# One table of letters for the order within 342 rounds, and the convolution in four streams

## The chip, the core and the metric

The kernel runs on one core of one Trainium2 chip. The metric is the device time of one execution in microseconds (us). Five engines work on their own instruction lists in a fixed order each and wait for one another by semaphores: TensorE (PE in the profile, its weight loads PEld), VectorE (DVE), ScalarE (ACT), GpSimd (POOL) and SyncE (SP). POOL, SP and ACT also issue DMA transfers. Since the lists are fixed when the program is built, an instruction that waits holds up all that stands behind it on its engine.

## The reference

Two independent results stand side by side in the output, over the same 2048 positions and 576 channels.

```python
# A: a state-space convolution. K has 576 filters of 2048 taps, summed over 128 states
P = exp(dt * (A_re + 1j * A_im)[:, :, None] * arange(L))
K = einsum("dn,dnl,dn->dl", C, P, dt * B).real
y = irfft(rfft(pad(u)) * rfft(pad(K)))[:L] + u * Dskip
# B: attention, 32 query heads of 18 with one key and one value head
q, k, v = x @ wq, x @ wk, x @ wv
o = softmax(q k^T * 18 ** -0.5) v
out = concatenate([y, o @ wo], axis=-1)
```

## The kernel before

**Attention.** The 2048 queries are cut into 4 chunks c of 512, the 32 heads into 16 pairs, the 2048 keys into 16 blocks kb of 128. One *tile* of scores is one head-pair member, one key block and one chunk: two matmuls (`s`, in half precision, K = 55) fill 128 x 1024 numbers of PSUM, ACT takes their exponentials in one instruction (`P`), and PE multiplies them by the values into `ops`, 8 instructions that the program calls a *product* being half of what two tiles need. There are 1024 tiles, `pairs` in the code, three PSUM buffers for scores (`NS = 3`) and eight buffers for exponentials (`NP = 8`). A *round* is three tiles; there are 342. Scores come from `scores`, exponentials from `exponentials`, products from `product`.

**What else PE does** is put between the products of the rounds, in pieces: the query projections (`q`, with the bound `up`), the output projections (`op`), and the convolution's groups. All of these use one PSUM bank, `ps_f`, the *filler bank*: a group must be evacuated by DVE before the next may start.

**The convolution** goes through 12 chunks k of 48 channels. `front(k)` makes the filters: DVE works out angles and decays, ACT takes sines and exponentials, and the tables `tab` give the taps by matmuls `kg`, evacuated to `ksb`. Sines need another table of functions on ACT than exponentials, so they are taken for two chunks at once: six *sine blocks*, the first before the loop and five within it, each of four sine instructions and two table loads. What the second chunk needs is parked in DRAM (`park<-two`) and loaded again. `back(k)` transforms the input (`hu`, `lu`) and the filter (`hk`, `lk`) by matmuls with `dft_sb`, multiplies the transforms on DVE in eight products and six additions (`acc`, `pt`), adds parts by accumulating DMAs on POOL's queue, recombines them (`sv`, `w`), transforms back (`iy`) and adds u times Dskip. Two streams run at a time: `back(k)` and `front(k + 1)`; `turn` starts the next two when both have ended.

**What sets the order.** The program is built by Python generators. `fill` is called before scores are due. It lets the streams (`prep`, `side` for projections, `conv`) take a step each while a credit lasts, which a planner works out from some twenty constants; the clock that it reads has one time each for PE, DVE and ACT, and guesses DMA landings as fixed spans (`K.t + 6.0`). The lines that decide:

```python
spare = credit - LEAST
if st is side and not (urgent or late or side.holds):
    spare -= SLOPE * max(ahead, 0.0)
elif st is side and side.holds:
    spare += HOLD
wait = then - K.t - (GAP_NEW if st is side and not urgent and not side.holds else GAP)
if st.go(self.step, max(spare, wait), holder()):
    more = True
    break
```

Behind the last tile, `conv.drain()` issues whatever is left of the convolution, and `finish` normalises the last heads (`rc_last`), ends the last output projection (`fin`) and stores it.

Of the kernel before, what the change touches and what calls it, by code (L numbers as in the profile page):

```python
# [25 lines left out]
KT = [(k * 128, 128) for k in range(5)]  # L26
DT = KT[:4] + [(512, 64)]
# [11 lines left out]
LIMIT = 60.0  # L39

# [5 lines left out]
RATE = 6.983  # L46
PACE = 1.7672
AHEAD = 0.4952
TOTAL = 604.4861
LAST = 813.2825  # L50
DEFER = 0.378
NAUG = 5
LEFT = 1.1655
CAP = 1.5491
DEBT = 0.6604
GROUP = 0.1377
HOLD = 0.3071
LEAD = 1.8204
MOST = 0.4269
LEAST = 0.3048  # L60
NEAR = 1.3779
SLOPE = 0.851
SOON = 1.3672
URGENT = 8.8421
BACK = 2
HELD = 0
GAP = 0.2663
GAP_NEW = 0.3191
# [13 lines left out]

class Clock:
# [6 lines left out]
    def __init__(self):  # L90
        self.t = self.v = self.a = 0.0
        self.work = 0.0
        self.s = [0.0] * NS
        self.fill = 0.0
        self.due = self.last = 1e9

    def near(self):

        return NEAR if self.t + SOON > min(self.due, self.last) else 0.0

    def pe(self, cost, *after):
        self.t = max(self.t, *after) + cost if after else self.t + cost

    def act(self, cost, after=0.0):
        self.a = max(self.a, after) + cost
        return self.a

    def filled(self):

        self.fill = self.v + 0.25  # L110
        self.due = 1e9

    def dve(self, n, rate, after):
        cost = 0.068 + rate * n + (0.119 if after else 0.0)
        self.v += cost
        self.work += cost


class Vector:
# [5 lines left out]
    def cost(self, rate, out, *ins, n=None):  # L125

        place = lambda x: (x.name, x.offset)
        self.k.dve(math.prod((n or out).shape[1:]), rate, self.last in [place(x) for x in ins if hasattr(x, "offset")])
        self.last = place(out)
# [9 lines left out]
    def tensor_scalar(self, out, src, *a, **k):  # L139
        self.cost(0.527e-3, out, src, *a)  # L140
# [18 lines left out]
class Stream:  # L159
# [26 lines left out]
    def go(self, step, credit, lock=None):  # L186

        k = self.k
        ready = self.ready if self.kind != "p" or self.holds else max(self.ready, k.fill)
        if not self.live or self.kind == "b" or self.kind == "p" and (credit <= 0 or k.t < ready or lock not in (None, self)):  # L190
            return False
        if self.kind == "v" and (k.t < self.ready or k.v > k.t + self.ahead - k.near()):
            return False
# [16 lines left out]
class Attention:  # L210
# [7 lines left out]
    def __init__(self, tc, ctx, aps, clock):  # L218
        self.tc, self.nc, self.a, self.k = tc, tc.nc, aps, clock
# [15 lines left out]
    def bank(self, n, name):  # L235
        self.k.pe(0.0, self.k.fill)
# [10 lines left out]
    def setup(self, tp, conv):  # L247
# [4 lines left out]
        self.sel = conv.con[:, 2 * NF:]  # L252
# [122 lines left out]
    def second(self):  # L375
# [3 lines left out]
        K.pe(0.86)  # L379
        self.last()  # L380
        K.pe(0.86)
        K.v = max(K.v, K.t)
# [6 lines left out]
    def maxima(self):  # L389
# [4 lines left out]
        K.pe(1.1)  # L394
        K.v = max(K.v, K.t)
# [4 lines left out]
    def values(self):  # L400
# [4 lines left out]
        K.pe(1.0)  # L405
        K.v = max(K.v, K.t)
# [8 lines left out]
    def qproj(self, c, m, xt):  # L415
# [5 lines left out]
        for f in range(n // 256):  # L421
            sl = slice(f * 256, f * 256 + 256)
            yield "p", K.fill, False
            ps = self.bank(256, f"q{c}_{m}_{f}")
            for k in range(5):
# [6 lines left out]
                K.pe(0.465)  # L432
                self.q_left -= 1
                self.units += 1
                K.due = K.t + 0.465 * (4 - k)
                if k < 4:
                    yield "p", 0.0, True
            K.v = max(K.v, K.t)
# [21 lines left out]
    def queries(self, c, m, qh, ql, aw):  # L460
# [18 lines left out]
        yield "p", max(K.v + 0.4, K.fill), False  # L479
# [10 lines left out]
        K.pe(0.15)  # L490
        K.v = max(K.v, K.t + 0.3)
# [33 lines left out]
    def scores(self, i, c, pr, kb, cost):  # L525
# [7 lines left out]
        K.pe(cost, K.s[i % NS])  # L533
        return ps, K.t + 0.27

    def exponentials(self, i, c, pr, kb, ps, ready, free):
        nc, K = self.nc, self.k
        K.s[i % NS] = K.act(0.925, max(ready, free)) + 0.1
# [7 lines left out]
    def gather(self, c, g, o_ps):  # L546
        nc = self.nc
        o_sb = self.p2.tile([P, CT], F32, tag="o", name=f"o{c}_{g}", bufs=1)
        self.k.v = max(self.k.v, self.k.t)
        self.V.tensor_copy(o_sb, o_ps)  # L550
        self.o_free = self.k.v + 0.3
        nc.sync.dma_start(self.od[c][g * P:(g + 1) * P, :], o_sb)

    def normalize(self, c, ms):
# [11 lines left out]
        yield "v", K.t + 6.0, False  # L566
# [6 lines left out]
        yield "v", K.v + 3.0, False  # L573
# [8 lines left out]
        for m in ms:  # L582
            mn = MT[m][1]
            yield "v", K.t + 5.0, False
            V.tensor_tensor(o[:mn, m, :], o[:mn, m, :], tiles[m][:mn, :], op=ALU.mult)
            self.scaled[m] = K.v + 0.3
# [3 lines left out]
    def outproj(self, c):  # L590
        nc, V, K = self.nc, self.V, self.k
        o = self.oT
        self.o_left += 40
        yield "p", max(self.scaled[4], K.fill), False
# [183 lines left out]
    def main(self, conv, flag):  # L778
# [81 lines left out]
        for r in range(0, len(pairs), NS):  # L860
# [45 lines left out]
            if r:  # L906
                fill(free())
# [643 lines left out]
```

## Time and profile before

| what | value |
|---|---|
| median of 3 runs | 1216.06 us (1213.11 to 1217.59) |
| the profiled execution | 1217.0 us, span 1215.2 us |
| busy PE / ACT / DVE / POOL | 1099.6 / 1035.3 / 961.1 / 95.5 us |
| mean granted clock of TensorE | 0.973 |
| DMA, all queues | 117.87 MB, mean 97 GB/s |

The span goes from the first to the last instruction of the profiled execution; the execution's own time is 1.8 us longer. An engine's busy time is the union of its instructions; matmuls overlap, and a PE that is busy is not PE at its peak. "Idle before" a group is the time that its engine stood still just ahead of it, with the one it waited for. A windows row gives, for one stretch, its length, the busy time and instruction count of each engine, the granted share of the TensorE clock, the share of the DMA engines and the rate.

### The profile page before, as it was taken

Reading aid. Unit: us, or ns where it says so; the run is one execution under the profiler, and the core shown is the slowest. Engines: PE = TensorE matmul, PEld = TensorE weight load, DVE = VectorE, ACT = ScalarE, POOL = GpSimd, SP = SyncE. Lnnn points to the kernel's source line nnn. Section 1 sums busy time; section 2 is a strip of 40 time slices with the busy share of each in tenths; the row PEclk is TensorE's granted clock in tenths of the full one; section 3 lists DMA queues with packets and bytes.
Section 4 is the critical chain, followed back from the end, with each engine's and each line's share of the span. In section 5 each row is a group of like instructions: output and inputs, shape, how many; then the busy total and the mean of one; then the engine's idle time right before and its main releaser. Section 6 shows DMA issues by size and latency. Waiting matters only on the chain. (4 is left out here: it accounts for less than half of the span.)

```text
span 1215.2 us, 41325 instructions
## 1 busy us (share of the span) xinstructions
PE 1099.6 (90%) x17974; PEld 534.7 (44%) x17974; DVE 961.1 (79%) x1722; ACT 1035.3 (85%) x1092; POOL 95.5 (8%) x151
## 2 busy tenths in 40 slices
PE   7999999899999899999989999986789998999924
PEld 2454454345445344545444545432344543454412
DVE  7868979977975885995989596873779589869875
ACT  5899899899889978999999999999689999999700
POOL 1010201110110100110010000020000000000000
PEclk9999999999999999999999999998899999999967
DMA  8432343343323324322341312232042124241122
GB/s 295 130 121 69 105 118 90 113 134 110 91 58 97 97 74 154 103 66 89 95 165 49 120 51 82 75 80 110 21 149 58 69 67 151 72 130 42 46 66 68
DMA packets 54253, 117.87 MB, mean 97 GB/s; under 512 B 7628, under 2 KB 24925, under 8 KB 52787
## 3 DMA queue, kind: packets, MB, share of 16 engines
q1 hardware_dynamic: 43571, 88.62, 21.6%
q0 software_dynamic: 10064, 26.19, 9.3%
q8 instruction: 143, 2.34, 0.8%
q10 hardware_dynamic: 432, 0.37, 0.1%
q14 instruction: 43, 0.35, 0.1%
HBM read 54.58 MB, written 41.46 MB: 79 GB/s over the span
## 5 line engine op out<-in xcount | busy, mean ns | idle before, releaser
L543 ACT ACTIVATE P<-s 128x1024 f32<-128x1024 f32 x992 | 938.9, 1036 | 95.5 <-PE s L532 90.0
L845 PE MATMUL ops<-P,v_sb 128*32 128x256 f32 x8192 | 536.6, 383 | 4.1 <-DVE o L137 3.6
L845 PEld LDWEIGHTS ops<-P,v_sb 128*32 128x32 f32 x8192 | 247.2, 110 | 187.3 <-issue 53.2
L532 PE MATMUL s<-aug,kaug 55*128 55x512 f16 x2048 | 303.2, 382 | 28.8 <-ACT P L543 25.6
L532 PEld LDWEIGHTS <-kaug 55*128 55x128 f16 x2048 | 95.2, 94 | 248.4 <-issue 202.1
L207 PE MATMUL op<-wo_sb,oT 126*32 126x288 f32 (+1 forms) x1128 | 84.7, 417 | 8.3 <-DVE ob L137 5.9
L207 PE MATMUL q<-x,wq_sb 128*32 128x256 f32 x1200 | 80.1, 395 | 7.4 <-DVE un L145 4.2
L137 DVE COPY ksb<-kg 128x192 f32<-128x192 f32 x48 | 17.4, 363 | 70.9 <-PE kg L1231 70.9
L207 PE MATMUL iy<-w,dft_sb 128*32 128x192 f32 x768 | 40.8, 344 | 24.6 <-DVE w L133 23.8
L133 DVE TENSOR_TENSOR tab<-tab,tt 128x576 f32<-128x576 f32 (+1 forms) x72 | 59.1, 821 | 1.5
L133 DVE TENSOR_TENSOR tab<-sum,r 128x576 f32<-128x576 f32 (+1 forms) x72 | 58.8, 817 | 0.0
L133 DVE TENSOR_TENSOR tt<-f,sum 128x576 f32<-128x576 f32 (+1 forms) x72 | 58.8, 817 | 0.0
L133 DVE TENSOR_TENSOR tab<-r,dif 128x576 f32<-128x576 f32 (+1 forms) x72 | 58.8, 816 | 0.0
L133 DVE TENSOR_TENSOR tab<-tab 128x576 f32<-128x576 f32 (+1 forms) x72 | 58.7, 815 | 0.0
L133 DVE TENSOR_TENSOR acc<-acc,pt 128x864 f32<-128x864 f32 (+2 forms) x72 | 54.4, 755 | 1.7
L133 DVE TENSOR_TENSOR pt<-us,ks 128x864 f32<-128x864 f32 (+2 forms) x72 | 54.2, 753 | 0.8
L207 PEld LDWEIGHTS q<-x,wq_sb 128*32 128x32 f32 x1200 | 36.8, 113 | 40.6 <-issue 13.2
L207 PEld LDWEIGHTS op<-wo_sb,oT 126*32 126x32 f32 (+1 forms) x1128 | 32.4, 111 | 47.3 <-issue 10.7
L1231 PE MATMUL kg<-tab 128*32 128x64 f32 x2304 | 42.9, 224 | 9.0 <-DVE tab L133 7.2
L1302 POOL DMA_DIRECT2D us<-us x12 | 6.7, 559 | 510.4 <-issue 227.0
L1231 PEld LDWEIGHTS kg<-tab 128*32 128x32 f32 x2304 | 37.8, 113 | 20.4 <-DVE tab L133 7.8
L676 ACT ACTIVATE o_last<-ops 128x256 f32<-128x256 f32 x2 | 0.8, 384 | 53.5 <-issue 51.9
(169 smaller groups left out, 1055.0 us busy)
## 6 DMA issues: line engine op xcount, KB each, us to landing
park<-two SPq DMA_DIRECT2D x6, 1944.0 KB
us<-us POOLq DMA_DIRECT2D x24, 384.0 KB, 3.9
od<-o SPq DMA_DIRECT2D x31, 256.0 KB
aug<-qd SPq DMA_DIRECT2D x124, 54.0 KB
u<-u SPq DMA_DIRECT2D x12, 480.0 KB
kd<-ksb SPq DMA_DIRECT2D x12, 384.0 KB
kt<-kd SPq DMA_DIRECT2D x48, 96.0 KB
ks<-ks POOLq DMA_DIRECT2D x12, 384.0 KB, 4.8
```

Source lines behind the costliest of these rows:

```text
L133: return self.v.tensor_tensor(out, a, b, **k)
L137: return self.v.tensor_copy(out, src)
L207: nc.tensor.matmul(ps[j:e], w[:, j:e], x, start=start, stop=stop, tile_position=(0, j))
L532: nc.tensor.matmul(ps[:, j, :], self.kaug[r, kb * P:(kb + 1) * P], t[r, :], start=True, stop=True)
L543: nc.scalar.activation(pt, ps, AF.Exp, scale=SCALE / UNIT ** 2)
L676: nc.scalar.activation(o_sb[:, half[f]], o_ps[:, half[f]], AF.Copy)
L845: nc.tensor.matmul(o_ps[32 * j:32 * j + 32, cs], self.v[:, kb, :], pts[2 * n + j // 2][:, j % 2, cs], start=(kb + f == 0), stop=(kb + f == ...
L1231: nc.tensor.matmul(ps[32 * g:32 * g + 32, d, :], t[:, :32], t[:, 32:], start=(j == 0), stop=(j == 1), tile_position=(0, 32 * g))
L1302: nc.gpsimd.dma_start(us[:, 0:4, :], us[:, 4:8, :])
```

## The change

The rounds, their number, the buffers and PE's groups stay. Four things differ.

1. **The clock models all engines.** Every read and write is entered by the cell of its tile, with a lag from each engine to the others; POOL's and SP's queues, DMA sizes and row lengths, instruction blocks of PE and the change between half and full precision have costs. Steps of streams become ready when that model says that their inputs are there (`K.at`).
2. **A letter for each round.** `fill` looks up a letter of `CODES` for round `i // 3`; it shifts the due time of the scores (0, -0.5, -0.25, +0.35, +0.8) and may put a product or a projection piece first. 172 of the 342 letters differ from `a`, which shifts nothing and puts nothing first. The planner's constants go.
3. **Four streams of the convolution** (`fronts`, `inputs`, `kernels`, `backs`), which may run chunks ahead of each other; two filter tiles `kt` may wait instead of one, and parked halves are loaded one step earlier (`resume`).
4. **DVE work goes to accumulating DMAs.** The six additions into `acc`, half of each transform's last step and half of the recombination become DMAs with `accum_op` on POOL's queue. The products are four wide ones (the first in three parts) instead of eight. u times Dskip becomes an addition to the filter's first tap; `out` is copied from `iy`.

```diff
-    def pe(self, cost, *after):
-        self.t = max(self.t, *after) + cost if after else self.t + cost
+    def pe(self, cost, out=None, ins=()):
+        self.fetch()
+        self.turn(0)
+        self.t = self.begin(1, self.t, out, tuple(ins)) + cost
+        self.done += cost
+        self.end(1, self.t, out, tuple(ins), 0.166 + HOP)
...
+    def dma(self, q, out, src, add):
+        t = self.begin(0, self.g if q == "g" else self.t, out, (src,) + ((out,) if add else ()))
+        if q == "g":
+            self.g = t = t + 0.56
...
+        t += (3.3 if q == "g" else LAND) + max(n * size / 1.9e5, n / min(run(out), run(src)) * 4.4e-3)
+        self.end(0, t, out, (src,), HOP)
...
+ORDERS = {chr(97 + 5 * j + i): (x, j) for i, x in enumerate((0.0, -0.5, -0.25, 0.35, 0.8)) for j in range(3)}
+CODES = (
+    "ehceinaaalaaaaaakcmagmaafmcmaamaaaablfgagggnkaaabljoahggaaaaaaaaaaaaaagbamgaabaaaaaanaeclaaacnmaamellacanaaaabkaaa"
...
+def order(r, a):
+    return CODES[r] if r < len(CODES) else "a"
...
+        def fill(i):
+
+            free = max(K.s[(i + j) % NS] - 0.225 * j for j in range(NS)) - 0.113
+            by, first = ORDERS[order(i // NS, self)]
+            late = free + SLACK + by
+            while True:
+                pump()
+                left = late - K.t
+                if first == 1 and behind < len(pairs) and ripe() <= K.t + 0.02 and left > ROOM:
+                    product()
+                    continue
+                if first == 2 and beside(left, True):
+                    continue
+                if conv.go(self.step, left + LET, holder()):
+                    continue
...
+                if behind < len(pairs) and ripe() <= K.t + 0.02 and left > ROOM:
+                    product()
+                    continue
...
-                    tt(t, at(us, 0, 4 - m), kb, op=ALU.mult)
-                    yield "v", 0.0, False
-                    tt(at(acc, m, 4), at(acc, m, 4), t, op=ALU.add)
-                    yield "v", 0.0, False
...
-        tt(ut, ut, dsk.unsqueeze(1).broadcast_to([P, 4, NE]), op=ALU.mult)
...
+            if m == 1:
+                nc.gpsimd.dma_start(acc[:, :, n:], t1, accum_op=ALU.add)
+        self.us_free = self.ks_free = True
+        nc.gpsimd.dma_start(t2[:, :, n:], t3, accum_op=ALU.add)
+        nc.gpsimd.dma_start(acc[:, :, 2 * n:], t2, accum_op=ALU.add)
+        nc.gpsimd.dma_start(acc[:, 0:4, :], acc[:, 8:12, :], accum_op=ALU.add)
+        yield "v", K.at(acc[:, 4:12, :]), False
+        tt(acc[:, 4:8, :], acc[:, 8:12, :], acc[:, 4:8, :], op=ALU.subtract)
...
+        self.streams = [Stream(g, self.k) for g in (self.fronts(), self.inputs(), self.kernels(), self.backs())]
```

Three places show what this does to the instruction lists. First PE behind the last scores but one, up to the first `fin` of `finish`: before, the last twelve rows of it,

```order
L1231 MATMUL kg_1_1_16307<-tab_1_15946 32x64 x24
L207 MATMUL hu_16342<-u_14737,dft_sb 32x192 x8
L207 MATMUL lu_16352<-u_14737,dft_sb 32x192 x8
L207 MATMUL hu_16363<-u_14737,dft_sb 32x192 x8
L207 MATMUL lu_16373<-u_14737,dft_sb 32x192 x8
L207 MATMUL hk_16392<-kt_16333,dft_sb 32x192 x8
L207 MATMUL lk_16402<-kt_16333,dft_sb 32x192 x8
L207 MATMUL hk_16413<-kt_16333,dft_sb 32x192 x8
L207 MATMUL lk_16423<-kt_16333,dft_sb 32x192 x8
L207 MATMUL iy_16477<-w_16468,dft_sb 32x192 x16
L207 MATMUL iy_16495<-w_16468,dft_sb 32x192 x16
L207 MATMUL fin_16518<-wo_sb,oT_14465 32x288 x8
```

and now, from the last scores on:

```order
L266 MATMUL s_15_15_16419<-aug_114,kaug 128x512
L266 MATMUL ops_7_16111<-P_14_14_16395,v_sb 32x256 x2
L266 MATMUL ops_7_16111<-P_15_14_16400,v_sb 32x256 x2
L266 MATMUL ops_7_16111<-P_14_15_16405,v_sb 32x256 x2
L266 MATMUL ops_7_16111<-P_15_15_16422,v_sb 32x256 x2
L266 MATMUL ops_7_16111<-P_14_15_16405,v_sb 32x256 x2
L266 MATMUL ops_7_16111<-P_15_15_16422,v_sb 32x256 x2
L266 MATMUL fin_16440<-wo_sb,oT_15394 32x288 x8
```

The whole of the last chunk's convolution has moved from behind the last scores to rounds ahead of them.

Second, PE at a sine block. The tile `s_14_5` is the last of the three score tiles that PE can give before ACT comes back from the sines (the fourth such block within the loop); before, this stood between it and the next scores, `s_15_5`:

```order
L845 MATMUL ops_7_12027<-P_14_1_12010,v_sb 32x256 x2
L845 MATMUL ops_7_12027<-P_15_1_12012,v_sb 32x256 x2
L845 MATMUL ops_7_12027<-P_14_1_12010,v_sb 32x256 x2
L845 MATMUL ops_7_12027<-P_15_1_12012,v_sb 32x256 x2
L845 MATMUL ops_7_12027<-P_14_2_12014,v_sb 32x256 x2
L845 MATMUL ops_7_12027<-P_15_2_12041,v_sb 32x256 x2
L845 MATMUL ops_7_12027<-P_14_2_12014,v_sb 32x256 x2
L845 MATMUL ops_7_12027<-P_15_2_12041,v_sb 32x256 x2
L845 MATMUL ops_7_12027<-P_14_3_12043,v_sb 32x256 x2
L845 MATMUL ops_7_12027<-P_15_3_12045,v_sb 32x256 x2
```

Now, at the fifth block within the loop, behind `s_15_15` (the list goes on with a product, the bound `up` and then scores):

```order
L266 MATMUL q_3_0_12737<-x_8711,wq_sb 32x256 x16
L266 MATMUL ops_7_12391<-P_14_12_12655,v_sb 32x256 x2
L266 MATMUL ops_7_12391<-P_15_12_12660,v_sb 32x256 x2
L266 MATMUL ops_7_12391<-P_14_13_12706,v_sb 32x256 x2
L266 MATMUL ops_7_12391<-P_15_13_12711,v_sb 32x256 x2
L266 MATMUL ops_7_12391<-P_14_13_12706,v_sb 32x256 x2
L266 MATMUL ops_7_12391<-P_15_13_12711,v_sb 32x256 x2
L266 MATMUL q_3_1_12801<-x_8711,wq_sb 32x256 x20
L266 MATMUL ops_7_12391<-P_14_14_12716,v_sb 32x256 x2
L266 MATMUL ops_7_12391<-P_15_14_12745,v_sb 32x256 x2
```

Projections have been kept for this place, where there were products alone.

Third, POOL's queue for a late chunk: before, from the transform of the input to the accumulation into `acc`,

```order
L1302 DMA us_15142<-us_15142 128x768
L1303 DMA us_15142<-us_15142 128x768
L1316 DMA ks_15324<-ks_15324 128x768
L1338 DMA acc_15615<-acc_15615 128x768
```

and now (`t` are the products that were `pt`):

```order
L251 DMA ks_13691<-ks_13691 128x2x192 x2
L251 DMA ks_13691<-ks_13691 128x768
L251 DMA acc_14222<-t_14223 128x12x144
L251 DMA t_14224<-t_14224 128x12x48
L251 DMA acc_14222<-t_14224 128x12x96
L251 DMA acc_14222<-acc_14222 128x768
L251 DMA us_14426<-us_14426 128x2x192 x2
L251 DMA us_14426<-us_14426 128x768 x2
L251 DMA acc_14222<-acc_14222 128x384 x2
L251 DMA w_14729<-w_14729 128x384
L251 DMA ks_14682<-ks_14682 128x2x192 x2
L251 DMA acc_14222<-acc_14222 128x2x192
```

Where four transfers served a chunk there are fifteen, of smaller rows, and those of neighbouring chunks stand between each other.

More of the change, by code (lines that the diff above doesn't have):

```diff
@@ L95, in __init__ @@
-        self.due = self.last = 1e9
-    def near(self):
-        return NEAR if self.t + SOON > min(self.due, self.last) else 0.0
-    def pe(self, cost, *after):
-        self.t = max(self.t, *after) + cost if after else self.t + cost
-    def act(self, cost, after=0.0):
-        self.a = max(self.a, after) + cost
-        return self.a
-    def filled(self):
[L110 to L116, printed above, removed]
+        self.table = None
@@ L478, in queries @@
             store(nc.gpsimd)
[L479 removed]
+        yield "p", K.at(aw), False
         up = self.bank(8, f"up{c}_{m}")
@@ L906, in main @@
-            if r:
-                fill(free())
-            c, g, kb, j = pairs[new[-1]]
-            self.group = (new[-1] + 1) // 32
+            while (i - NP) // 2 >= behind // 2:
+                product()
+            pts[i] = self.exponentials(i, c, 2 * g + j, kb, *ps, read.get((i - NP) // 2, 0.0))
+            done[i] = K.a
+            if j == 0:
+                continue
+            self.group = (i + 1) // 32
             self.fetch(self.group)
```

655 lines of the change are left out of this document (377 added, 278 removed).

## The prediction

> **What bounds the kernel now.** I read the page first, for shares; then the windows, to cut the span into stages; then the waits, and the timeline where a window showed a loss.
>
> ```profile
> span 1215.2 us, 41325 instructions
> ...
> PE 1099.6 (90%) x17974; PEld 534.7 (44%) x17974; DVE 961.1 (79%) x1722; ACT 1035.3 (85%) x1092; POOL 95.5 (8%) x151
> ...
> PE   7999999899999899999989999986789998999924
> ...
> ACT  5899899899889978999999999999689999999700
> ```
>
> PE is the fullest engine, ACT next; both are full nearly everywhere except in the last slices and around slice 28. Windows (length; busy time with instructions of PE, weight loads, DVE, ACT, POOL; granted clock; DMA share; GB/s) for the stages: from the first exponential to the last, the drain behind it, the finish.
>
> ```profile
> 26.20:1147.30 1121.10, 1051.33 (x17282) 513.03 (x17282) 898.94 (x1606) 1020.45 (x1074) 87.26 (x134) 0.98 0.31 94
> 1147.30:1199.30 52.00, 18.88 (x392) 11.01 (x387) 34.52 (x59) 0.15 (x1) 3.13 (x4) 0.70 0.22 54
> 1199.30:1215.20 15.90, 9.42 (x152) 5.25 (x144) 7.54 (x13) 0.77 (x2) 0.00 (x0) 0.95 0.28 104
> ```
>
> So 1121.1 us hold all 1024 exponentials, 52.0 us hold none, with PE at 18.9 of 52. I then cut the 1121.1 into sixteen stretches of 64 exponentials. Five hold a block of sines (ACT leaves the exponentials there); these rows, with the first of the sixteen, a plain one, and the sum over the seven plain ones in which PE is at least 96% busy, starting at 96.0, 241.6, 456.3, 521.5, 661.9, 727.1 and 1083.6:
>
> ```profile
> 26.20:96.00 69.80, 68.23 (x1134) 33.98 (x1134) 49.39 (x99) 63.43 (x64) 7.16 (x13) 0.98 0.40 129
> 162.10:241.60 79.50, 70.73 (x1168) 34.83 (x1160) 66.89 (x127) 70.63 (x76) 10.42 (x16) 0.98 0.36 105
> 377.10:456.30 79.20, 74.21 (x1120) 35.45 (x1112) 68.78 (x121) 70.45 (x75) 5.47 (x8) 0.98 0.29 87
> 587.00:661.90 74.90, 69.30 (x1123) 34.10 (x1112) 67.17 (x124) 70.06 (x73) 7.77 (x12) 0.98 0.34 104
> 943.00:1019.60 76.60, 72.01 (x1174) 34.55 (x1166) 56.21 (x98) 70.72 (x76) 2.27 (x3) 1.00 0.28 90
> 793.40:876.00 82.60, 59.58 (x802) 26.14 (x795) 51.12 (x82) 69.07 (x73) 3.76 (x5) 0.90 0.22 69
> ...
> 661.90:727.10 65.20, 64.95 (x1098) 32.00 (x1098) 51.45 (x83) 61.00 (x65) 2.91 (x3) 1.00 0.30 90
> 1083.60:1147.30 63.70, 61.82 (x950) 28.09 (x950) 61.13 (x108) 59.98 (x64) 3.14 (x4) 1.00 0.21 53
> ...
> sum 456.10, PE 447.58 PEld 220.85 DVE 377.84 ACT 424.79 POOL 37.95; mean PE 63.94 PEld 31.55 DVE 53.98 ACT 60.68 POOL 5.42
> ```
>
> A plain stretch takes 456.1 / 7 = 65.2 us at 98% of PE: PE sets it. The four sine stretches with work on PE (mean 1146 matmul records) take 310.2 / 4 = 77.6 us, of which ACT is busy 70.5. The fifth, at 793.4, takes 82.6 us with only 802 records: PE has too little to do and ACT too much, and then PE is held up.
>
> ```profile
> 843.71 0.61 PE L532 MATMUL s<-aug,kaug 55*128 55x512 f16 x2 [5.79 <-ACT P L543]
> 846.08 2.61 PE L845 MATMUL ops<-P,v_sb 128*32 128x256 f32 x24
> 847.44 0.43 DVE L137 COPY tab<-r 128x192 f32<-128x192 f32 x2 [0.75 <-DMA park<-two]
> 859.66 0.65 PE L1231 MATMUL kg<-tab 128*32 128x64 f32 x15 [7.24 <-DVE tab L133]
> ```
>
> PE stands 5.79 us while ACT does its sines, runs 24 product records in 2.61 us at a lowered clock, and at 859.66 stands 7.24 us more, because a kg group comes in its order ahead of scores, while its table waited for a parked tile to come back. A stall of PE in a fixed order is a stall of ACT.
>
> **The change, part by part, against the profiled execution (1217.0 us; span 1215.2 and 1.8 around it; the median of the runs is 0.9 lower).** The order's own counts are the same on PE: 4096 product matmuls, 2048 of scores, 680 of q, 640 of op and fin, 1152 of kg, 768 of the forward and 384 of the inverse transforms. PE's work moves; it does not shrink.
>
> (1) The drain. In the new order nothing of the convolution stands behind the last scores: two halves of a product, then finish.
>
> ```profile
> 1145.91 0.64 PE L845 MATMUL ops<-P,v_sb 128*32 128x256 f32 x8
> 1151.56 0.88 PE L1231 MATMUL kg<-tab 128*32 128x64 f32 x48 [0.68 <-DVE u L133]
> 1193.25 2.79 PE L207 MATMUL iy<-w,dft_sb 128*32 128x192 f32 x32 [23.50 <-DVE w L133]
> 1198.82 0.40 DVE L675 TENSOR_SCALAR rc_last<-ops 128x256 f32<-128x256 f32 x1
> ```
>
> Finish begins with rc_last at 1198.82 and ends with the span, 16.4 us. Two product halves cost 0.64 + 0.43 and the handover some 0.2: the 67.9 us behind 1147.3 become 1.3 + 16.4 = 17.7. What hid nothing there, a chain of PE, DVE and DMA steps, is now beside exponentials; should it come out late again, each us is paid again.
>
> (2) Its PE work comes into the loop: 392 records. A record costs 0.054 us in a run of them:
>
> ```profile
> 817.86 2.37 PE L845 MATMUL ops<-P,v_sb 128*32 128x256 f32 x40
> 820.91 1.50 PE L845 MATMUL ops<-P,v_sb 128*32 128x256 f32 x24
> ```
>
> (2.37 - 1.50 for 16 more; kg records are shorter, so this is a little dear.) The mean load is then (17282 + 392) / 16 = 1105 records a stretch. Since the letters and the four streams spread it (by the order's counts no stretch is short of work any more), I price every stretch alike. Eleven plain ones: 65.2 plus 7 records over the 1098 of the quoted row, 0.4, makes 65.6; 721.6 in all, and 4.6 more for the first (69.8 against 65.2), whose front I see unchanged. Five sine stretches: 77.6 minus 41 records, 2.2, makes 75.4; 377.0. Loop: 1103.2 against 1121.1. The 17.9 us come from the starved stretch and from three plain ones below 96%.
>
> (3) The finer order itself. Behind the last scores that PE can give ahead of a sine block, the order has now 4.2 to 6.3 us of its work in each of the five places (its counts times 0.054 to 0.06 a record), against 2.2 to 8.0 before: the worst place is mended, and there is no clear gain over the four good ones. In plain stretches the bounds are nothing, and all of them as short as 63.7, the shortest row: 1.5 x 11 = 17. In sine stretches nothing, and ACT's own 70.5: 5 x 5 = 25, so -42 to 0, and a loss can come only with wrong landings, which is (5). I take -1.0 for each plain stretch, nearest the short row since rounds now end on the scores' own due time, and -1 for each sine stretch: -16.
>
> (4) DVE does less. Removed per chunk: six additions into acc, two of the four last steps of each transform, half of the sv and w steps, the product with Dskip.
>
> ```profile
> L133 DVE TENSOR_TENSOR acc<-acc,pt 128x864 f32<-128x864 f32 x24 | 25.3, 1053 | 0.4
> ...
> L133 DVE TENSOR_TENSOR us<-scu 128x384 f32<-128x384 f32 x48 | 23.5, 550 | 0.0
> ...
> L133 DVE TENSOR_TENSOR acc<-acc,pt 128x576 f32<-128x576 f32 x24 | 18.1, 755 | 0.6
> ...
> L133 DVE TENSOR_TENSOR u<-u 128x768 f32<-128x768 f32 x12 | 11.4, 950 | 0.0
> L133 DVE TENSOR_TENSOR acc<-acc,pt 128x288 f32<-128x288 f32 x24 | 11.0, 457 | 0.7
> ```
>
> That is 25.3 + 18.1 + 11.0, then 8 steps of 0.55 in each of twelve chunks (52.8), then 11.4 less 24 small tap additions of some 0.15 (7.8): 115 us, a tenth of DVE. PE, not DVE, sets the plain stretch, where its 2% idle is 1.3 us: the gain is between nothing and 11 x 1.3 = 14. I take nothing, since the cover is PE itself, 98% busy.
>
> (5) What DVE gives up goes to DMAs on POOL's queue, all but one per chunk accumulating: fifteen per chunk against four, 132 more, and seven places per chunk where DVE or PE waits in its order for one, 84 in all. Other queues keep their number; qd and sd stores now stand behind the new ones on POOL's queue.
>
> ```profile
> L1338 POOL DMA_DIRECT2D acc<-acc x12: 844/885/946, 144.0 to 1187.7; - x12
> ...
>   DVE sv L133: 2.9, 2
> ...
> DMA to landing us min/median/max: 3.9/4.3/9.4
> ```
>
> Issuing costs POOL 132 x 0.885 = 117 us on an engine 8% busy: covered. The waits: twelve such landings cost DVE 2.9 us, 0.24 each; 84 of them 20 us of DVE. A lower end below nothing I exclude, a wait gives nothing back. Upper end: one landing per chunk at the row's maximum, 9.4 - 4.3 = 5.1 late, passed on in full: 61. The order leaves work between issue and use, as before, so I take the near end, and a third of it reaching PE: +7. Rows of 192 and 576 bytes, which the new ones have, occur in no accumulating DMA here.
>
> Sum: 26.2 + 1103.2 - 16 + 7 + 17.7 = 1138.1 of span; 1139.9 with the 1.8; less 0.9, 1139.
>
> **A rule that speaks against it.** The twelve issues of the row took 844 to 946 ns, beside a DVE that was busy 80% of the loop (898.94 of 1121.10); twelve others, of the accumulation into us, spread more:
>
> ```profile
> L1303 POOL DMA_DIRECT2D us<-us x12: 842/878/1476, 110.6 to 1166.7; - x12
> ```
>
>  The Trainium skill's page SBUF — State Buffer, section SBUF: two separate sides, says that DMAs issued from GpSimd stall for descriptors while DVE runs a two-port operation, such as an fp32 copy within SBUF. The trace shows little of it: one issue in 24 took 0.6 us over the median, and none of the others more than could matter. By the rule these DMAs would come late whenever DVE copies, and the time would go towards the slower rival below.
>
> **The rivals.** (a) Accumulating DMAs come late: DVE stands in its order, evacuations of the one filler bank behind it, PE behind that, then ACT. Place: the seven waits of each chunk. For: many more transfers share the 16 engines, three pieces are larger or finer than any accumulated now. Against: 0.24 us a wait now. Half of the upper end gives 1139 - 7 + 31 = 1163; slower than now it is from (1216 + 7 - 1139) / 12 = 7.0 us a chunk on, and at 8 us it gives 1228. (b) The order is as good as its bounds: -42 and no lateness, 1139 + 16 - 42 - 7 = 1106. For: plain rows of 63.7 exist; against: PE has 98% there. (c) ACT becomes the bound: its 1020.45 busy in the loop lies 74 below the 1094 that I forecast for it, so this happens only in single stretches; it would give some 1139 + 10, for a stretch like the one at 793.4 left over. (d) The letters do nothing on the chip, since their model's durations are not the trace's: then the plain order of the same streams runs; the drain still goes, +16: 1155.
>
> **How the numbers follow.** My case, 1120 to 1165: 0.48; (d) and (c), in the same stretch: 0.10 and 0.02. (b), below 1120: 0.17. (a) mild, 1165 to 1209: 0.15. Within 0.5% (about 6 us, what a measurement of this kernel can tell from no change): 0.03. (a) in full, slower: 0.05. Faster by over 0.5% is 0.48 + 0.12 + 0.17 + 0.15 = 0.92. The range takes in my case, (d), (c), (b) as worked out and the lower half of (a), and leaves out about 0.05 below and 0.15 above: 1104 to 1185.
>
> **What the profile would show.** Right: the last exponential's end about 18 us before the span's; no kg, hu, hk or iy behind it; sixteen stretches of 63 to 67, five of them 72 to 77; no PE wait over 6 us in the loop; DVE some 850 busy; POOL some 210. Wrong: DVE waiting for accumulating DMAs for more than 40 us in all, PE waiting for evacuations behind it, aug tiles late after qd stores, or convolution work behind the last scores.

## The result, and the profile after

The changed kernel takes 1211.22 us (median of 20 runs, 1201.34 to 1215.21) beside 1215.93 us (20 runs, 1213.11 to 1219.74): a ratio of 0.9943, 95% interval 0.9928 to 0.9959. It is 4.7 us faster; 1139 was forecast. The profiled execution took 1213.16 us, with a span of 1211.3.

The page's first lines, and its line on POOL's DMA queue (packets, MB, share of 16 engines' span):

```profile
span 1211.3 us, 41437 instructions
...
PE 1116.6 (92%) x17974; PEld 540.3 (45%) x17974; DVE 861.4 (71%) x1545; ACT 1035.9 (86%) x1092; POOL 265.9 (22%) x283
...
PE   7999999999997999999969897999999699999997
...
DMA  8342597872785862768845735862958732958301
...
q0 software_dynamic: 87440, 66.31, 36.7%
```

PE is full to the last slice, where it showed 2 and 4 before: the drain is gone. DVE is 100 us less busy. POOL's queue carries 87440 packets, and its share was 9.3% before. The windows of the loop and of what follows it, in the same columns as before:

```profile
26.00:1194.20 1168.20, 1085.27 (x17654) 529.42 (x17652) 833.24 (x1485) 1021.15 (x1074) 260.86 (x270) 0.98 0.59 126
1194.20:1211.30 17.10, 10.40 (x156) 5.31 (x156) 8.00 (x14) 0.84 (x3) 0.00 (x0) 0.93 0.21 73
```

Behind the last exponential stand 17.1 us, and 67.9 before: 50.8 gained. The loop is 1168.2, and was 1121.1: 47.1 lost. The forecast for the loop was 1103.2 - 16 + 7 = 1094.2, so the whole miss, 74 us in this execution, lies in the loop. Four of its sixteen stretches of 64 exponentials, none of which holds a block of sines:

```profile
26.00:105.20 79.20, 72.91 (x1126) 35.09 (x1128) 54.19 (x108) 63.56 (x65) 9.43 (x14) 0.94 0.42 127
...
608.90:693.10 84.20, 69.76 (x1128) 34.97 (x1120) 61.96 (x108) 60.92 (x67) 16.72 (x16) 0.90 0.57 117
...
918.50:994.90 76.40, 65.06 (x1046) 30.77 (x1047) 60.03 (x108) 60.47 (x65) 18.68 (x20) 0.93 0.66 143
1130.50:1194.20 63.70, 62.64 (x858) 28.46 (x854) 15.53 (x33) 60.35 (x64) 1.20 (x1) 1.00 0.13 38
```

The second and third are plain stretches with 84.2 and 76.4 us in place of 65: PE has about the mean of 1103 records, and stands 14 and 11 us. The first, 79.2, holds something that the new accumulating DMAs did not bring: from 26 to 40 us the granted clock was 0.76, and the first of those DMAs is issued at 70.1. The last has only 858 records and 15.5 us of DVE. What DVE waited for on DMAs (us in total, times, longest):

```profile
DVE acc L301 <- DMA acc<-t: 19.4, 3, 14.9
DVE oT L301 <- DMA db<-rden: 18.8, 9, 4.3
...
DVE w L301 <- DMA acc<-acc: 13.0, 4, 7.7
...
DVE ks L305 <- DMA ks<-ks: 12.2, 6, 4.1
...
DVE qh L309 <- DMA qd<-qh: 7.5, 2, 4.8
...
DVE r__6116 L301 <- DMA sum__6117<-park: 3.9, 1, 3.9
```

The three rows on accumulations sum to 44.6 us, where the row of before had 2.9. `oT` waited for no `db` before. `qh` waits for the stores `qd`, which stand behind accumulations on POOL's queue.

One such wait in full. POOL's own rows first, as the timeline has them from 586 us on (start, length, what ended the idle time before it):

```profile
586.92 2.75 POOL L251 DMA_DIRECT2D us<-us  x2
596.30 0.60 POOL L251 DMA_DIRECT2D us<-us  x1 [6.63 <-DMA us<-us]
600.09 0.85 POOL L251 DMA_DIRECT2D us<-us  x1 [3.19 <-DMA us<-us]
600.71 0.87 POOL L251 DMA_DIRECT2D sd<-sh  x1
601.34 2.02 POOL L251 DMA_DIRECT2D acc<-acc  x2
602.44 1.79 POOL L251 DMA_DIRECT2D w<-w  x1
602.98 2.36 POOL L251 DMA_DIRECT2D qd<-qh  x2
```

The copy within `us` waits on POOL for the accumulations ahead of it, the next accumulation waits for the copy, and the two into `acc`, which are another stream's, stand behind them in POOL's order. They are issued at 601.34. Then they share the 16 engines with the parked tiles that SP has just asked for; the windows there (the last three columns are the granted clock, the DMA share by the packets' own times, so it may pass 1, and GB/s):

```profile
600.00:606.00 6.00, 5.63 (x156) 3.03 (x150) 3.73 (x8) 5.81 (x7) 5.77 (x8) 1.00 0.80 169
606.00:614.00 8.00, 6.20 (x90) 2.55 (x82) 0.25 (x2) 7.56 (x9) 1.57 (x3) 1.00 1.07 298
614.00:620.00 6.00, 0.00 (x0) 0.00 (x0) 5.93 (x12) 2.02 (x3) 1.90 (x2) 0.58 0.64 153
```

and what came of it on DVE, PE and ACT:

```profile
613.88 0.56 DVE L301 TENSOR_TENSOR w<-acc 128x384 f32<-128x384 f32 x1 [7.75 <-DMA acc<-acc]
...
614.86 1.44 DVE L301 TENSOR_TENSOR r__8576<-r__8576,sum__8577 128x1248 f32<-128x1248 f32 x1
...
616.23 1.44 DVE L301 TENSOR_TENSOR f__8575<-f__8575,sum__8577 128x1248 f32<-128x1248 f32 x1
...
620.41 0.67 DVE L305 COPY o<-ops 128x512 f32<-128x512 f32 x1
...
621.13 4.36 PE L266 MATMUL ops<-P,v_sb 128*32 128x256 f32 x40 [7.42 <-DVE o L305]
...
625.91 1.94 ACT L714 ACTIVATE P<-s 128x1024 f32<-128x1024 f32 x2 [9.89 <-PE s L266]
```

DVE stands 7.75 us. Behind the late step wait, in DVE's order, the work of the front and then the copy of `o`, without which PE cannot begin the next group of products: PE stands 7.42 us. The granted clock falls to 0.58 meanwhile, and is 0.56 from 620 to 626, so 40 records then take 4.36 us where the prediction's row had 2.37; ACT stands 9.89 us.

The Trainium skill's page DMA: Bandwidth & Descriptors, section Issuing engines are not separate DMA queues, says that transfers asked for by different engines run on the same 16 DMA engines and interleave. The trace agrees: a share of 1.07 from 606 to 614, with packets of both queues in it.

### The profile page after: what moved, and what is told of

Read it like the earlier page. It is cut to its first block, busy times and chain, and to the rows that moved or that the text cites. A ratio compares the mean times of both kernels' runs of the same rounds, so it can differ in the third digit from the quotient of the medians.

```text
span 1211.3 us, 41437 instructions
## 1 busy us (share of the span) xinstructions
PE 1116.6 (92%) x17974; PEld 540.3 (45%) x17974; DVE 861.4 (71%) x1545; ACT 1035.9 (86%) x1092; POOL 265.9 (22%) x283
## 3 DMA queue, kind: packets, MB, share of 16 engines
q0 software_dynamic: 87440, 66.31, 36.7%
## 4 chain that ended last, share of the span: by engine, by line
PE 30%; DVE 19%; DMA 15%; issue 6%; ACT 2%; POOL 1%; SPq 0%; DVEq 0%; POOLq 0%; ACTq 0%
PE ops L266 13%; PE s L266 7%; DVE tab L301 5%; DMA acc<-t 4%; PE op L266 3%; DMA db<-rden 2%; ACT P L714 2%; DMA ks<-ks 2%; DVE t L301 2%; PE kg L266 2%; PE iy L266 1%; DMA us<-us 1%; DVE tt L301 1%; DVE ks L301 1%; DVE acc L301 1%
## 5 line engine op out<-in xcount | busy, mean ns | idle before, releaser
L266 PE MATMUL ops<-P,v_sb 128*32 128x256 f32 x8192 | 554.6, 387 | 25.0 <-DVE o L305 14.9
L266 PE MATMUL q<-x,wq_sb 128*32 128x256 f32 x1360 | 89.7, 393 | 7.2 <-DVE ql L321 5.9
L251 POOL DMA_DIRECT2D acc<-acc x48 | 52.3, 1186 | 175.1 <-DMA acc<-t 84.7
L251 POOL DMA_DIRECT2D ks<-ks x36 | 39.6, 1252 | 225.2 <-DVE ks L301 210.8
L251 POOL DMA_DIRECT2D acc<-t x24 | 43.8, 1824 | 202.2 <-issue 67.6
L251 POOL DMA_DIRECT2D us<-us x48 | 50.0, 1215 | 115.1 <-DMA us<-us 89.7
L266 PE MATMUL kg<-tab 128*32 128x64 f32 x2304 | 44.0, 226 | 15.5 <-DVE tab L301 11.3
L301 DVE TENSOR_TENSOR t<-us,ks 128x1728 f32<-128x1728 f32 (+2 forms) x36 | 47.3, 1348 | 1.5 <-DMA outa<-out 1.5
L251 POOL DMA_DIRECT2D qd<-qh x46 | 30.4, 810 | 58.8 <-DVE qh L309 54.1
L301 DVE TENSOR_TENSOR ks<-ks 128x384 f32<-128x384 f32 (+2 forms) x60 | 41.8, 713 | 0.8
L712 ACT ACTIVATE P<-s,nb 128x1024 f32<-128x1024 f32 x32 | 33.2, 1115 | 9.6 <-PE s L266 9.4
```

Source lines behind the costliest of these rows:

```text
L251: return self.q.dma_start(out, src, **k)
L266: return self.e.matmul(out, w, x, **k)
L301: return self.v.tensor_tensor(out, a, b, **k)
L712: nc.scalar.activation(pt, ps, AF.Exp, scale=SCALE / UNIT ** 2, bias=self.nb)
```

## Experiments

**T1**: the accumulating DMAs come late and cost the difference. **T2**: the order itself is long on the chip, since the planner's durations are not the chip's. The medians of before beside the runs lie between 1214.5 and 1216.7; ratios are to those.

### Without the new accumulating DMAs

```diff
-    def dma_start(self, out, src, **k):
+    def dma_start(self, out, src, kept=False, **k):
         self.k.dma(self.name, out, src, "accum_op" in k)
+        if "accum_op" in k and not kept:
+            return
         return self.q.dma_start(out, src, **k)
```

The three that the kernel before had are marked `kept`; the first line still tells the planner of all, so the order stays.

> Leaves out the eleven new accumulating DMAs of each chunk (the convolution's sums are incomplete); PE, DVE and ACT keep the changed kernel's order instruction for instruction, since the planner is still told of the eleven. Theory T1 (the order is as good as forecast, and the new accumulating DMAs, which come late on the chip, cost the difference): the forecast without its term for lateness, 1132, at most 1150; DVE waits for accumulations under 5 us in all. Rival T2 (the order itself, whose durations are a planner's and not the chip's, makes the loop long): still over 1190. Rival T3 (half and half): 1160 to 1180.

1169.27 us (1168.04 to 1169.97), ratio 0.9622 (0.9606 to 0.9638). The same PE, DVE and ACT lists are 42 us faster, and no wait of DVE for an accumulation is left: T1's mechanism is there, with six times its booked price. But 1169 is not 1132, nor under 1150; it lies in the third case, half and half. Some 37 us are lost without them. The page's lines and the loop:

```profile
span 1168.0 us, 41137 instructions
...
PE 1107.8 (95%) x17974; PEld 537.2 (46%) x17974; DVE 858.4 (73%) x1545; ACT 1035.6 (89%) x1092; POOL 93.5 (8%) x151
```

```profile
26.80:1151.40 1124.60, 1075.22 (x17654) 526.17 (x17652) 830.29 (x1485) 1020.77 (x1074) 88.79 (x139) 0.99 0.31 95
```

From the changed kernel to this run DVE's waits for DMAs go from 82 us to 29. PE stands 34.5 us less (94.7 of the span, then 60.2), and its work takes 8.8 us less at a mean granted clock of 0.986 in place of 0.976. So, beside 53 us that DVE waits less, PE stands less by some two thirds of them, and its shorter work makes the rest of the 43 us between the two spans. Some 5 us of the difference of these two executions lie in the first stretch (79.2 against 74.5), where the clock falls ahead of any of the eleven (0.76 against 1.00 from 26 to 40 us); the profile of the next run, whose eleven move next to no data, has the same 0.76 and a first stretch of 80.2. How many of the 20 runs have this is not known, so the 42 may hold some of it.

### The same DMAs with next to no data

```diff
+        if "accum_op" in k and not kept:
+            out, src = (t[(slice(0, 1),) + tuple(slice(0, n) for n in t.shape[1:-1]) + (slice(0, 1),)] for t in (out, src))
```

> The same order, and the eleven accumulating DMAs are still issued and waited for, but each adds only one element of each of its 2 to 12 rows of one partition (the sums are incomplete): issue, fixed latency and the places of the waits stay, the data and nearly all packets go. T1a (the packets' own time on the shared 16 engines makes them and others late): as without them, 1130 to 1155. T1b (issuing on POOL and the queue order on it, fixed latency): near the changed kernel, 1185 to 1211.

1167.47 us (1164.72 to 1172.85), ratio 0.9603 (0.9583 to 0.9622): outside the 1130 to 1155 of T1a, but level with leaving them out, as T1a says. POOL is still 203.1 us busy (265.9 in the changed kernel, 93.5 without the eleven), since the issues are shorter with less data. These issues, the fixed latency and the waits' places cost nothing; what goes with the data does. The issues and landings of `acc` here, and in the changed kernel:

```profile
L253 POOL DMA_DIRECT2D acc<-acc x48: 771/883/1549, 152.8 to 1092.4; - x48
...
L253 POOL DMA_DIRECT2D acc<-t x24: 801/962/1092, 146.2 to 1059.4; - x24
...
DMA to landing us min/median/max: 1.8/3.1/8.3
```

```profile
L251 POOL DMA_DIRECT2D acc<-acc x48: 842/1179/2130, 168.7 to 1131.9; - x48
...
L251 POOL DMA_DIRECT2D acc<-t x24: 1785/1820/1889, 145.2 to 1108.5; - x24
...
DMA to landing us min/median/max: 3.3/6.5/12.8
```

With their data, a landing takes 6.5 us at the median, 3.1 without.

### Without the three large ones

```diff
+        if leave:
+            return
...
-                nc.gpsimd.dma_start(acc[:, :, n:], t1, accum_op=ALU.add)
+                nc.gpsimd.dma_start(acc[:, :, n:], t1, accum_op=ALU.add, leave=True)
...
-        nc.gpsimd.dma_start(t2[:, :, n:], t3, accum_op=ALU.add)
-        nc.gpsimd.dma_start(acc[:, :, 2 * n:], t2, accum_op=ALU.add)
+        nc.gpsimd.dma_start(t2[:, :, n:], t3, accum_op=ALU.add, leave=True)
+        nc.gpsimd.dma_start(acc[:, :, 2 * n:], t2, accum_op=ALU.add, leave=True)
```

> Leaves out only the three large accumulating DMAs of each chunk (t1 into acc, t3 into t2, t2 into acc; the sums are incomplete), the other eight new ones stay; order instruction for instruction as changed. Leaving out all eleven gave 1169, the changed kernel 1211. T1c (the three hold 55,296 of 77,000 new packets and stand in front of the others on POOL's queue, so the others are late behind them): 1170 to 1182. T1d (each of the eight waits costs by itself): 1190 to 1205.

1178.06 us (1175.47 to 1181.57), ratio 0.9706 (0.9671 to 0.9740): T1c. 33 of the 42 us go with the three, 9 with the eight others. In the changed kernel POOL itself stood 84.7 us for `acc<-t` and 60.0 for `t<-t`, with everything behind it:

```profile
POOL us L251 <- DMA us<-us: 89.7, 21, 7.5
POOL acc L251 <- DMA acc<-t: 84.7, 12, 10.0
...
POOL acc L251 <- DMA t<-t: 60.0, 6, 11.9
```

### All letters plain

```diff
 def order(r, a):
-    return CODES[r] if r < len(CODES) else "a"
+    return "a"
```

> All 342 letters are the plain one, the rest as changed. If the letters do on the chip what they are there for: slower than the changed kernel by the 16 us that the prediction took for the finer order, 1227. T1: the lateness outweighs what a letter can set, within 10 us of the changed kernel, 1201 to 1221. T2 in its strong form (the letters fit the planner's durations and not the chip's): faster, under 1200.

1241.80 us (1236.19 to 1245.47), ratio 1.0217 (1.0179 to 1.0254). The letters are worth 31 us on the chip, twice the 16 of the prediction's rival (d); without them the change is slower than before. T2 in its strong form falls.

### The additions back on DVE

```diff
-        nc.gpsimd.dma_start(acc[:, 4:6, :], acc[:, 6:8, :], accum_op=ALU.add)
+        tt(acc[:, 4:6, :], acc[:, 4:6, :], acc[:, 6:8, :], op=ALU.add)
...
```

> The eleven additions of each chunk go back to DVE as tensor_tensor, with the streams, the planner and the letters of the changed kernel; the planner makes a new order with them. DVE's busy time goes up by the 115 us that the prediction booked at nothing, to some 970. T1: the drain stays gone and the lateness goes: 1140 to 1165. T2: 1190 or more. If DVE's load is what the planner cannot place, PE waits for DVE and it is 1180 or more with few waits for DMAs.

1211.67 us (1208.42 to 1212.80), ratio 0.9964 (0.9951 to 0.9977): by the time T2 or the third case. The planner made a new order here, so the run does not test the order of the changed kernel. DVE's waits for DMAs are few, 14 us in all, and the windows fit the third case, DVE's load that this planner does not place:

```profile
25.90:1167.30 1141.40, 1077.36 (x17486) 522.01 (x17484) 910.05 (x1587) 1020.52 (x1074) 87.48 (x137) 0.99 0.31 93
1167.30:1211.00 43.70, 21.88 (x325) 12.51 (x324) 21.62 (x32) 0.91 (x3) 0.85 (x1) 0.78 0.15 48
```

The loop is 26.8 us shorter than in the changed kernel and the tail 26.6 longer: the drain is back. There PE waited for DVE's last sums of a chunk:

```profile
1182.32 1.51 PE L266 MATMUL iy<-acc,dft_sb 128*32 128x192 f32 x16 [13.77 <-DVE acc L301]
```

### A planner that is told of the transfers

```diff
+        took = rows * (27 + 0.0765 * row if add else 6 + 0.038 * row) * 1e-3 / 16
...
-            self.g = t = t + 0.56
+            s = max(t + LATE_G, self.lines[0])
+            self.g = t = t + 0.8 + 0.65e-3 * rows
...
-        t += (3.3 if q == "g" else LAND) + max(n * size / 1.9e5, n / min(run(out), run(src)) * 4.4e-3)
...
+        t = max(s + took + SHARE * min(took, max(0.0, other - s)), t + LATE_S)
+        self.lines[i] = t
```

With plain letters, then with letters found anew on it:

> The accumulating DMAs stay as in the changed kernel. The planner is told what the traces show of transfers: those of one queue follow one another on the 16 engines, the two queues slow each other, an accumulating packet takes 27 ns and 0.0765 ns a byte, POOL's issue takes 0.8 us and 0.65 ns a row. All letters are the plain one, so it compares with the run of plain letters, 1242. T1 (lateness that the planner does not know of makes the loss): 42 us or more of it go, 1180 to 1200, and DVE waits for DMAs for under 30 us. If knowing it helps nothing, since there is nothing else to put in between: over 1225.

> As the run before it, with 342 letters found anew on the planner that is told of the transfers. The letters of the change were worth 31 us against the plain ones; if new ones on the better planner are worth as much: 1150 to 1170. If a letter's worth is an accident of one order: no better than the plain letters within 10 us.

1230.42 us (1226.74 to 1239.76), ratio 1.0145 (1.0087 to 1.0203), and 1221.29 us (1218.15 to 1227.09), ratio 1.0051 (1.0020 to 1.0081). Both hit the second of their cases: the knowledge brings 11 us of 42, the new letters 9 more, and the kernel is 10 us slower than the changed one. What the planner was told is not enough to take the lateness away. In the second of these DVE still waits:

```profile
DVE w L316 <- DMA acc<-acc: 32.3, 10, 10.2
...
DVE acc L316 <- DMA acc<-t: 20.5, 5, 6.3
```

So I left the eleven out of that order, instruction for instruction:

> The order of the planner that is told of the transfers, with its letters (1221), instruction for instruction, without the eleven new accumulating DMAs of each chunk (the sums are incomplete). If the accumulating DMAs cost more in this order than in the changed kernel's, since it leaves less between issue and use: 1155 to 1172, so 50 us or more for the eleven. If the order is what is bad: over 1180.

1164.34 us (1161.00 to 1165.77), ratio 0.9574 (0.9545 to 0.9603). The order is good, better than the changed kernel's by 5 us without them, and the eleven cost 57 us in it. What the told planner still has wrong about their landings, and whether an order without lateness exists for them, I did not settle.

### All on DVE, told planner

As in the diff of the additions above, on the planner that is told, with letters found for it, with plain letters, and with letters found for a planner whose transfers land later:

> All eleven additions back on DVE (as in the run that gave 1212), the planner told of the transfers, letters found anew for it. In that run the drain had come back (44 us behind the last exponential) and the loop took 1141. T1: no drain, a loop near 1120, few waits for DMAs: 1150 to 1170. If DVE at some 975 busy sets the pace: 1185 or more, with PE waiting for DVE and DVE for nothing.

> All eleven additions on DVE, the planner told, all letters plain: beside 1176 this is the worth of letters where few transfers come late. If it is as large as with the accumulating DMAs (31): 1207. If letters were mostly repairing lateness there: within 10 us of 1176.

> As the run of 1176, but the planner takes each transfer on SP's queue to land 0.7 us later (2.4 in place of 1.7) and each on POOL's queue 0.2 later, and its letters are found for that. In the run of 1176 DVE still waited 13.5 us for db and 5.8 for acc. If these waits are what holds it up: 1160 to 1170, with DVE's waits for DMAs halved. If later landings only move the waiting to the planner's own holes: 1176 or more.

1176.24 us (1171.69 to 1177.23), ratio 0.9670 (0.9633 to 0.9706); 1197.43 us (1196.07 to 1198.59), ratio 0.9834 (0.9809 to 0.9859); 1174.80 us (1170.88 to 1176.88), ratio 0.9655 (0.9630 to 0.9679). The first lies between its cases. Letters are worth 21 us here, between theirs. The margin takes DVE's waits for DMAs from 26 us to 11, as the first of its cases said, and the time stays, at the edge of the second (1176 or more): in these orders those waits were covered. Each of the three is faster than both kernels. The last one's loop and tail:

```profile
26.00:1146.30 1120.30, 1066.79 (x17561) 521.79 (x17562) 920.83 (x1606) 1019.89 (x1074) 88.77 (x138) 0.99 0.31 96
1146.30:1169.00 22.70, 15.43 (x256) 8.32 (x248) 8.14 (x14) 0.84 (x3) 0.00 (x0) 0.95 0.16 56
```

DVE is 88 us busier in the loop than in the changed kernel, and the loop is 47.9 us shorter; it is level with that of the first run without the eleven (1124.6). The orders differ, so this does not show that DVE's load is free: with the told planner, leaving the eleven out gave 1164.3, and 10 to 12 us less than the two with letters here. The tail is 5.6 us longer, with 256 records of PE left to it in place of 156.

### Three on DVE, eight on POOL

The three large additions of each chunk go back to DVE, on the told planner with letters found for it:

> Only the three large additions of each chunk go back to DVE, the eight smaller ones stay accumulating DMAs; the planner is told of the transfers, letters found for it. DVE gets some 50 us less to do than with all eleven (1176). Leaving out the three large ones moved 33 of the 42 us that all eleven cost, so if what is left of lateness, 9 us, is all that the eight cost, this is level with 1176 or up to 9 slower: 1172 to 1188. If DVE's load binds with all eleven, this is faster: 1150 to 1168. If the chain of small accumulations at each chunk's end is late even to the planner that is told (as DVE's 32 us of waits for acc<-acc in the run of 1221 say): 1190 or more.

1206.41 us (1202.52 to 1211.35), ratio 0.9914 (0.9882 to 0.9946): the third of the cases, but DVE's waits for `acc<-acc` are only 10.0 us. It is PE that waits, for the last accumulation of a chunk and with no releaser shown:

```profile
PE iy L281 <- issue: 11.7, 3, 4.3
PE iy L281 <- DMA acc<-acc: 7.8, 3, 5.0
```

The same order without the eight:

> The order with the three large additions on DVE (1206), instruction for instruction, without the eight smaller accumulating DMAs (the sums are incomplete). Beside the changed kernel's order the eight cost 9 us (1178 against 1169). If their cost hangs on the order: 1160 to 1178, so some 30 us for the eight here. If it is the order: 1195 or more.

1178.51 us (1177.42 to 1182.38), ratio 0.9693 (0.9669 to 0.9718). The eight cost 28 us here and 9 in the changed kernel's order: no one price per DMA fits both. That it hangs on what stands behind each is argued, not shown.

### Without late db loads

```diff
-            nc.sync.dma_start(tiles[m][:mn, :], rd[m0 // DH:(m0 + mn) // DH, :].unsqueeze(1).broadcast_to([mn // DH, DH, CT]))
+            nc.sync.dma_start(tiles[m][:mn, :], rd[m0 // DH:(m0 + mn) // DH, :].unsqueeze(1).broadcast_to([mn // DH, DH, CT]),
+                              instead=self.a["wo"][m0 // DH:(m0 + mn) // DH, 0:CT].unsqueeze(1).broadcast_to([mn // DH, DH, CT]))
```

The planner is told of `rd` as before; what is issued is `instead`, on top of leaving the eleven out.

> As the run without the eleven DMAs (1169), and the db tiles (the reciprocals that normalize multiplies by) are loaded from the weights in place of what was just stored, so no load waits for the chain of stores and loads ahead of it (the attention's rows are scaled wrongly, the sums are incomplete); PE, DVE and ACT keep the order. In the run of 1169 DVE waited 19.2 us for db in 7 waits, and two plain stretches, 592.9 to 669.9 and 886.0 to 955.5, took 12 and 5 us more than the forecast's 64.6. If the late db loads make those: 1152 to 1160, both stretches under 68. If DVE's waits there are covered and the stretches are long for other reasons (the parked tiles, which came 4.6 us late at 595.8): 1165 to 1170.

1163.88 us (1161.73 to 1167.96), ratio 0.9589 (0.9558 to 0.9620): between the two cases, 5.4 us. Of its two plain stretches, the one that took 77.0 takes 72.0, still not under 68, and the one that took 69.5 takes 67.7. The row of the run without the eleven, and of this one:

```profile
592.90:669.90 77.00, 68.49 (x1130) 33.61 (x1120) 60.95 (x103) 60.90 (x67) 3.99 (x6) 0.93 0.25 77
```

```profile
591.90:663.90 72.00, 66.95 (x1128) 33.55 (x1120) 61.72 (x107) 60.94 (x66) 4.02 (x7) 0.98 0.27 81
```

DVE waits 2.5 us for a parked tile in the first of these stretches here, 4.6 in the run of 1169. Whether the parked tiles make the rest was not tried: their loads can't be left out without a race.

## Why the prediction was wrong, step by step

| step | forecast | measured | by |
|---|---|---|---|
| (1) behind the last exponential | 17.7 | 17.1 | the windows |
| (2) and (3), the loop without lateness | 1087.2 | some 1117.6 | the run without the eleven and without late db |
| late db loads | not priced | 5.4 | two runs, 1169.3 against 1163.9 |
| (4) DVE's lighter load | 0 | at most some 12, not separated from the order | the told planner, 1164.3 without the eleven sums, 1176.2 with them on DVE |
| (5) late accumulating DMAs | 7 | 42 | two runs, 1211.2 against 1169.3 |

The miss is 72 us by the medians: 42 - 7 of (5), 5 of db, and 32 of (2) and (3) (30.4 in the profiled execution, 2 us shorter than its median).

**(5) is the term that was mis-sized, by 35 us.** The mechanism of rival (a), its place and its chain (DVE in order, evacuations, PE, ACT) are what the trace shows; the sign of "wrong", DVE waiting over 40 us for accumulations, came, at 44.6. The bounds, 0 to 61, held the 42, which may include some of the 5 us of the first stretch. What failed is the choice of the near end from a row of 0.24 us a wait: that row was measured on a queue 9.3% busy, and the change itself made it 36.7%. Twelve landings among four DMAs a chunk were no rate for eleven more in the same queue. And a third of DVE's waiting was booked as reaching PE: some two thirds did, 34.5 of 53 us, and the granted clock, which the sum left out, fell with it.

**(3) did not come, and (2) was priced too evenly.** In the run with neither the eleven nor late db, the five sine stretches sum to 374.1 us (forecast 372.0), the first takes 74.6 (69.2: its front does change), and the ten other plain ones 668.9 (646.0, at 64.6). The third sine block is cut by a border between two stretches, so that some of it counts among the plain ones. The letters are worth 31 us, but against the plain letters of the same planner, not against the kernel before: its good stretches were already at 65.2, and the shortest row, 63.7, which (3) leaned on, held only 950 records. That no stretch is short of work was wrong: the last has 858 records where the mean is 1103. The 245 missing are spread over the others, some 0.9 us each (245 / 15 x 0.054), and the last still takes 63.7. The 16 us of (3) and these 13 make nearly the 30.4, but that is arithmetic: no run takes (2) and (3) apart, and the first stretch, 5 us over, has no cause shown.

**The rest.** (1) was right to 0.6 us, with no convolution behind the last scores. Of (4), DVE's busy time was right, 861.4 (forecast 850); that nothing is gained is not shown. POOL is 265.9 busy, not 210: issuing took 1.8 us for the 1536-row transfers, not 0.885. Of the rivals, (b) and (c) did not come; (d), at 1155, was refuted by the run of plain letters. The fifth sine stretch of before, 82.6, is 75.2 now, near the 74.4 forecast.

**The rule that spoke against the change** (the Trainium skill, SBUF — State Buffer, section SBUF: two separate sides) pointed to the right DMAs, and issues did lengthen: the accumulations into `us` and their copies take up to 2506 ns, 897 where the eleven are left out. (Of the issues before, three of 24 were 0.5 to 0.6 us over the median, not one.) The run with next to no data keeps every instruction of DVE and every issue, though shorter ones (`acc<-t` 962 ns at the median for 1820), and costs nothing. Issues stuck behind two-port operations would need the data's descriptors to show; no run here takes these apart from the packets' own time, so the rule is neither shown nor excluded.

```profile
L251 POOL DMA_DIRECT2D us<-us x48: 579/1023/2506, 70.1 to 1063.4; - x48
```

```profile
L253 POOL DMA_DIRECT2D us<-us x24: 541/706/897, 68.3 to 1010.6; - x24
```

## What to carry to other kernels

When a change moves work to a queue, price its waits by the load that the queue will have, not by a row from the load that it has; and book a wait of an in-order engine that evacuates the only free bank as reaching PE in large part: two thirds here, and none where the order covers it, as the run with the margin shows. Work that moves off an engine which is not the bound gains little: here moving DVE's 115 us cost some 42 us of lateness, and giving them back, with the order found again, gives 1174.8 us, 0.9655 of the kernel before. A finer order is worth what it is measured against: 31 us against its own plain form was far less against the tuned one.

## What was not expected of the hardware

- An accumulating packet within SBUF takes about twice a plain one of the same bytes: 264 ns in the kernel before (253 in the changed one) at 3072 bytes, where the plain copies within `us` took 246 (234) for packets of 6144, and SP's packets of 3072, to or from DRAM, 122. Accumulating rows of 192, 384, 576 and 768 bytes took 41, 55, 75 and 84 ns at the median, so, as an estimate, some 27 ns and 0.0765 ns a byte.
- POOL's issue grows with the rows: 842 ns at the least for `acc<-acc`, 1785 to 1889 for the 1536 rows of `acc<-t`, and 962 at the median for the same issues with next to no data. Issues right behind one another overlap and lengthen (601.34 to 603.36 and 602.44 to 604.23 in the rows above). The stores `qd<-qh` of 128 KB, which add nothing up but stand in the same queue, landed in 2.2 us at the median before and in 5.4 after.
